# Key transposes in order, preparation and loads most of a batch ahead, attention up to 2.2 batches ahead

## The chip, the cores and the metric

The kernel runs on one core of one Trainium2 chip. The metric is the device time of one execution in microseconds; for the kernel before, three runs are shown, and their median is 276.2 us.

## The reference

Eight batches of 576 tokens and 8 heads of 64 numbers go through a pooled attention, and its output, 4608 tokens of 512 numbers, through a layer of eight experts of which each token uses one.

```python
# q, k, v: (8, 8, 576, 64)
k_p = k.reshape(B, H, 72, 8, D).mean(axis=3)         # keys and values pooled by 8: 72 groups
v_p = v.reshape(B, H, 72, 8, D).mean(axis=3)
attn = softmax(q @ k_p.T / sqrt(D))
x = (attn @ v_p) as rows of tokens, 4608 x 512
logits = (x / |x|) @ (expert_emb / |expert_emb|).T / tau
expert_idx = argmax(logits); gate_w = softmax(logits)[expert_idx]
out[t] = gate_w * (relu(x[t] @ w1[e]) @ w2[e])       # e = expert_idx[t]; w1 512 x 1024, w2 1024 x 512
```

## The kernel before, in words

All of a batch's tokens are multiplied with the weights of one expert, the one that the routing finds most often; a loop at the end repairs batches in which tokens chose others, and on this data it runs no round. So the work of batch b is: load its inputs, prepare them, do the attention, find the expert, load that expert's two weights, and do the expert layer (the FFN).

**Inputs** (`load_qkv`): keys, queries and values are loaded by three transfers in GpSimd's DMA queue, which also turns float32 into fp16. The pool `inp` has two buffers of each, so the inputs of batch b+2 can be loaded only when those of b have been used. **Weights** (`load_w`): two transfers of 1 MB (as fp16) in the same queue, three buffers each.

**Preparation**, all on VectorE. Keys (`kproc`): two additions, a transpose in blocks of 32x32, and a last addition that leaves `kT`, the pooled keys. The transpose (line 163) writes its result so that the two halves of a pooled group come to lie side by side, and the last addition (line 168) adds neighbours. Queries (`qtr`): two transposes. Values (`vadd`): three additions, which leave `vpx`.

**Attention**: `score` is 8 matmuls and two exponentials on ScalarE, four times a batch; `pv` is 48 small matmuls, and `xtr` normalizes and transposes their result on VectorE into `xt_all`, three times a batch. `square` on ScalarE, `sumsq` on GpSimd and `ssq` on TensorE form the tokens' norms; `gate_steps` makes the gate of it (a power on GpSimd, then VectorE and an exponential). `route` and `expert` find the expert's index, which GpSimd reads into a register before it can issue the weights' loads.

**The expert layer** (`ffn_steps`): 8 steps `hgrp` (w1, 8 matmuls each, ReLU on ScalarE, or on VectorE for w = 1 and 5), then 8 steps `yblk` and one `ylast` (w2, then the gate's scaling and the stores on SP's queue).

**The order** is written out by hand; each engine works through its instructions in the order in which the program names them. After a prologue, the program goes through the steps of the expert layers. A step at place x (batch number plus the done part of the layer) is preceded by all attention steps whose place is less than `lead(x)`. The places are numbers in `attn_steps`: batch plus 0.00 for the keys, 0.16 to 0.40 for the scores, and so on to 0.97 for the expert. `lead(x)` is x plus 1.5, growing to 1.7. The prologue holds all the attention of batch 0 and about half of that of batch 1.

In the profiles, names of buffers are the program's: `k` is the transposed key tile `k4`, `pa` any of the four PSUM tiles, `w` the weights, `at` the exponentials, `x_sb` and `xt_all` the attention's output.

## Time and profile before

| | |
|---|---|
| runs shown | 275.04, 276.2, 277.79 us; median 276.2 |
| profiled execution | 274.75 us, span 273.1 us, mean granted TensorE clock 0.882 |
| busy, share of the span | TensorE matmul 189.7 us (69%), VectorE 184.8 (68%), ScalarE 103.1 (38%), GpSimd 68.8 (25%) |
| DMA | 40.81 MB, mean 149 GB/s |

Busy times are averages over the whole span. An engine with 68% may still hold up the others in every batch, which is seen only in stretches of one batch and in the chain of waits: that chain is followed back from the last instruction, at each step to what released it. Adjacent pieces of it are on the path that set the end. The granted clock is TensorE's, as a share of full speed.

### The profile page before, as it was taken

To read this page: it belongs to the slowest core of one execution; us is meant where nothing else is said; L and a number is where in the kernel's file an instruction comes from. 1 tells how busy PE (TensorE), PEld (TensorE's weight loads), DVE (VectorE), ACT (ScalarE), POOL (GpSimd) and SP (SyncE) were. 2 spreads that over 40 slices of the span, in tenths; PEclk is the share of its full clock that TensorE was granted. 3 is DMA by queue.
4 is the path that set the end of the run, shared out by engine and by line. 5 is a ranking of instruction groups with operands and counts; after the bars stand their busy time and mean duration, and the time that the engine had idled before them with its cause. 6 is when DMAs were issued, how large, how long until landed. Compare 5 with 4: busy or idle time off the path is not lost.

```text
span 273.1 us, 6241 instructions
## 1 busy us (share of the span) xinstructions
PE 189.7 (69%) x2614; PEld 111.0 (41%) x2615; DVE 184.8 (68%) x353; ACT 103.1 (38%) x180; POOL 68.8 (25%) x75
## 2 busy tenths in 40 slices
PE   0144356682999189963999099927997599999930
PEld 0123234451268023750467035712475147758510
DVE  3969973559379963999299946997399929624110
ACT  2033513261427234371627053533427152815310
POOL 8204064150010900155012801081013301341000
PEclk9999997597799759995999779975999599999995
DMA  5998999991032899549985899479963954397340
GB/s 102 204 186 133 208 200 205 210 187 30 4 84 91 151 209 184 176 72 205 216 158 137 170 216 212 132 123 209 209 176 52 203 99 136 49 197 193 99 131 20
DMA packets 19582, 40.81 MB, mean 149 GB/s; under 512 B 2520, under 2 KB 8152, under 8 KB 18528
## 3 DMA queue, kind: packets, MB, share of 16 engines
q0 software_dynamic: 14096, 30.94, 62.0%
q1 hardware_dynamic: 5116, 8.86, 9.7%
q10 hardware_dynamic: 340, 0.59, 0.7%
q8 instruction: 21, 0.34, 0.5%
q14 instruction: 9, 0.07, 0.1%
HBM read 61.88 MB, written 9.44 MB: 261 GB/s over the span
## 4 chain that ended last, share of the span: by engine, by line
PE 57%; DVE 34%; ACT 2%; DMA 2%; issue 1%; ACTq 0%; POOLq 0%
PE pa L408 25%; PE pa L390 17%; DVE k L163 8%; DVE kT L168 6%; PE pa L203 5%; DVE qT L177 4%; PE pa L223 4%; PE pa L431 3%; DVE xt_all L240 2%; DVE x_sb L237 2%; DMA kk<-in_k_dram 2%; PE pa L276 2%; DVE kk L158 2%; DVE hT L399 2%; ACT at L209 2%; DVE ks L161 1%
## 5 line engine op out<-in xcount | busy, mean ns | idle before, releaser
L408 PE MATMUL pa<-w,hT 128*128 128x512 f16 x256 | 71.2, 427 | 0.0
L390 PE MATMUL pa<-xt_all,w 128*128 128x288 f16 x512 | 70.5, 294 | 0.0
L209 ACT ACTIVATE at<-pa 72x576 f16<-72x576 f32 x64 | 37.3, 642 | 81.1 <-PE pa L203 81.0
L203 PE MATMUL pa<-qT,kT 32*72 32x288 f16 x256 | 19.2, 386 | 57.9 <-DVE qT L177 57.3
L390 PEld LDWEIGHTS <-w 128*128 128x128 f16 x512 | 48.9, 100 | 14.8 <-issue 1.9
L408 PEld LDWEIGHTS <-hT 128*128 128x128 f16 x256 | 24.6, 105 | 36.2 <-issue 17.1
L397 ACT ACTIVATE hT<-pa 128x576 f16<-128x576 f32 x48 | 30.2, 646 | 18.9 <-PE pa L390 18.6
L203 PEld LDWEIGHTS <-kT 32*72 32x72 f16 x256 | 7.1, 132 | 72.3 <-DVE qT L177 45.1
L253 POOL TENSOR_TENSOR sq<-sq 128x1152 bf16<-128x1152 bf16 (+1 forms) x16 | 29.7, 1858 | 17.8 <-ACT sq L248 9.9
L349 POOL TENSOR_TENSOR ssq<-ssq,half_c 128x5 f32<-128x5 f32 x8 | 9.6, 1195 | 96.6 <-DVE ssq L265 96.6
L421 DVE TENSOR_SCALAR y_sb<-pa,gm 128x512 f32<-128x512 f32 x16 | 11.8, 735 | 32.1 <-PE pa L408 32.1
L240 DVE STREAM_TRANSPOSE xt_all<-x_sb 128x768 f16<-128x768 f16 x24 | 23.5, 979 | 0.8
L419 ACT ACTIVATE y_sb<-pa,gm 128x512 f32<-128x512 f32 x16 | 11.0, 688 | 34.4 <-DVE y_sb L421 29.0
L237 DVE TENSOR_TENSOR x_sb<-pa,rc 128x768 f16<-128x768 f32 x24 | 23.0, 957 | 0.8
L248 ACT ACTIVATE sq<-xt_all 128x576 bf16<-128x576 f16 x32 | 20.5, 677 | 6.8 <-DVE xt_all L240 6.8
L163 DVE STREAM_TRANSPOSE k<-ks 128x576 f16<-128x576 f16 x8 | 21.8, 2720 | 0.3
L177 DVE STREAM_TRANSPOSE qT<-qq 128x1152 f16<-128x1152 f16 x16 | 21.2, 1349 | 0.0
L100 POOL DMA_DIRECT2D w<-in_moe_w_dram x8 | 5.0, 621 | 61.7 <-DVE kk L158 38.8
L399 DVE TENSOR_SCALAR hT<-pa 128x576 f16<-128x576 f32 x16 | 11.8, 738 | 11.0 <-PE pa L390 11.0
L223 PE MATMUL pa<-vpx,at 72*32 72x65 f16 x1152 | 16.7, 205 | 2.7 <-ACT at L209 2.0
L223 PEld LDWEIGHTS <-at 72*32 72x32 f16 x1152 | 12.8, 102 | 8.9 <-issue 6.1
L235 DVE RECIPROCAL rc<-pa 128x12 f32<-128x12 f32 x24 | 5.3, 222 | 15.6 <-PE pa L223 15.5
(84 smaller groups left out, 156.7 us busy)
## 6 DMA issues: line engine op xcount, KB each, us to landing
w<-in_moe_w_dram POOLq DMA_DIRECT2D x16, 1024.0 KB, 10.8
out_dram<-y_sb SPq DMA_DIRECT2D x30, 256.0 KB
kk<-in_k_dram POOLq DMA_DIRECT2D x8, 576.0 KB, 14.4
vv<-in_v_dram POOLq DMA_DIRECT2D x8, 576.0 KB, 21.1
qq<-in_q_dram POOLq DMA_DIRECT2D x7, 576.0 KB, 17.4
out_dram<-y_sb SPq DMA_DIRECT2D x15, 64.0 KB
qq<-in_q_dram POOLq DMA_DIRECT2D x2, 288.0 KB, 8.3
out_dram<-y_sb ACTq DMA_DIRECT2D x2, 256.0 KB
```

What stands on the lines that cost most here:

```text
L163: nc.vector.transpose(out=k4.rearrange("p w r (i m) -> p m w r i", m=T // 4), in_=ks.rearrange("p m (w r i) -> p m w r i", w=2, r=2))
L177: nc.vector.transpose(out=qT.rearrange("p w r (t i) -> p t w r i", i=16), in_=qq.rearrange("p t (w r i) -> p t w r i", w=2, r=2))
L203: nc.tensor.matmul(out=pS[a // 2][0:G, (a % 2) * 512:(a % 2) * 512 + HALF], lhsT=kT[rows, w, r, :], rhs=qT[rows, w, r, :], start=(w == 0), ...
L209: nc.scalar.activation(out=at, in_=pS[i][0:G].rearrange("g (a c) -> g a c", a=2)[:, :, 0:HALF], func=AF.Exp, scale=escale)
L223: nc.tensor.matmul(out=px[ts(a, 32), c0:c0 + D + 1], lhsT=st['at', half, r, a // 2][:, a % 2, ts(blk, 32)], rhs=st['vpx'][:, 2 * a + r, 0: ...
L237: nc.vector.tensor_tensor(out=x_sb, in0=pxv[:, :, :, 0:D], in1=rc.unsqueeze(3).to_broadcast([128, 2, 6, D]), op=ALU.mult)
L240: nc.vector.transpose(out=xt_all[:, b].rearrange("p w (t l) -> p t w l", l=32)[:, ts(u, 6)], in_=x_sb.rearrange("p b j d -> p (b j d)").re ...
L248: nc.scalar.activation(out=st['sq'][:, w], in_=xt_all[:, b, w], func=AF.Square)
L253: nc.gpsimd.tensor_tensor(out=sq[:, 0:n], in0=sq[:, 0:n], in1=sq[:, n:2 * n], op=ALU.add)
L390: nc.tensor.matmul(out=ph[:, half * 512:half * 512 + HALF], lhsT=w1v[:, kk, w // 2, w % 2, :], rhs=xt()[:, kk, ts(half, HALF)], start=(kk ...
L397: nc.scalar.activation(out=dst, in_=src, func=AF.Relu)
L408: nc.tensor.matmul(out=py, lhsT=st['hT'][:, w // 2, w % 2, ts(c, 128)], rhs=w2[:, w // 2, w % 2, :], start=(w == 0), stop=(w == 7))
```

## The change

The diff, without a few lines that only follow from it (new bounds of loops and blank lines):

```diff
-    LEAD = 1.7
+    LEAD = 2.2
@@ kproc
-            k4 = att.tile([128, 2, 2, 2 * G], FP16, name="k4")
-            nc.vector.transpose(
-                out=k4.rearrange("p w r (i m) -> p m w r i", m=T // 4),
-                in_=ks.rearrange("p m (w r i) -> p m w r i", w=2, r=2))
+            k4 = att.tile([128, T // 4, 2, 2, 16], FP16, name="k4")
+            nc.vector.transpose(out=k4.rearrange("p m w r i -> p (m w r i)"),
+                                in_=ks.rearrange("p m d -> p (m d)"))
             kT = att.tile([128, 2, 2, G], FP16, name="kT")
-            k42 = k4.rearrange("p w r (g s) -> p w r g s", s=2)
-            nc.vector.tensor_tensor(out=kT, in0=k42[:, :, :, :, 0], in1=k42[:, :, :, :, 1],
-                                    op=ALU.add)
+            kTv = kT.rearrange("p w r (i m) -> p (w r) i m", i=8)
+            k4v = k4.rearrange("p m w r (i s) -> p (w r) i m s", s=2)
+            for dst, a, b_ in ((slice(0, 4), (slice(0, 8, 2), 0), (slice(1, 8, 2), 0)),
+                               (slice(4, 5), (slice(8, 9), 0), (slice(0, 1), 1)),
+                               (slice(5, 9), (slice(1, 9, 2), 1), (slice(2, 9, 2), 1))):
+                nc.vector.tensor_tensor(out=kTv[:, :, :, dst], in0=k4v[:, :, :, a[0], a[1]],
+                                        in1=k4v[:, :, :, b_[0], b_[1]], op=ALU.add)
@@ qtr
-            qT = att.tile([128, 2, 2, TH * 16], FP16, name="qT")
+            qT = att.tile([128, 2, 2, TH * 16], FP16, name="qT", bufs=4)
@@ expert
             weights[b] = load_w(e_val)
-            if b + 2 < B:
-                load_qkv(b + 2)
@@ places of the steps (attn_steps)
-        K = [(0.00, kproc)]
-        Q = [(0.07, lambda: qtr(0)), (0.18, lambda: qtr(1))]
-        V = [(0.24, lambda: vadd(0)), (0.30, lambda: [vadd(1), vadd(2)])]
-        SC = [(0.16 + 0.08 * i, lambda h=i // 2, r=i % 2: score(h, r)) for i in range(4)]
-        P = [(0.50 + 0.11 * u, lambda u=u: pv(u)) for u in range(3)]
-        X = [(0.505 + 0.11 * u, lambda u=u: xtr(u)) for u in range(3)]
-        R = [(0.92, lambda: route(0, NC)), (0.97, lambda: expert(list(range(NC))))]
-        A = [(0.80 + 0.04 * w, lambda w=w: square(w)) for w in range(4)]
-        A += [(0.99, sumsq)]
+        def more():
+            if b + 2 < B:
+                load_qkv(b + 2)
+        V = [(-0.80, lambda: vadd(0)), (-0.73, lambda: [vadd(1), vadd(2)])]
+        K = [(-0.64, kproc)]
+        Q = [(-0.52, lambda: qtr(0)), (-0.40, lambda: qtr(1))]
+        L = [(-0.36, more)]
+        SC = [(0.28 + 0.12 * i, lambda h=i // 2, r=i % 2: score(h, r)) for i in range(4)]
+        P = [(0.74 + 0.12 * u, lambda u=u: pv(u)) for u in range(3)]
+        X = [(0.745 + 0.12 * u, lambda u=u: xtr(u)) for u in range(3)]
+        R = [(1.10, lambda: route(0, NC)), (1.16, lambda: expert(list(range(NC))))]
+        A = [(1.02 + 0.05 * w, lambda w=w: square(w)) for w in range(4)]
         if b < 2:
-            R = [(0.5, lambda: route(0, 1)), (0.5, lambda: expert([0])),
-                 (0.85, lambda: route(1, 4)), (0.90, recount)]
+            R = [(0.87, lambda: route(0, 1)), (0.92, lambda: expert([0])),
+                 (1.10, lambda: route(1, 4)), (1.16, recount)]
@@ gate_steps
         def norm():
-            st['emit_ssq']()
...
-        return [norm, prob, gate]
+        return [st['sumsq'], st['emit_ssq'], norm, prob, gate]
@@ hgrp
-            if w % 4 != 1:
+            if w != 5:
                 nc.scalar.activation(out=dst, in_=src, func=AF.Relu)
@@ the prologue and the merge with the expert layers
+        def lead(pos):
+            return pos + min(1.2 + 0.25 * pos, LEAD)
         run(a0['K'], a0['Q'][:1], a0['S'][:2], a0['V'])
         emb_transposed(4)
-        run(a0['P'][:1], a0['X'][:1], a0['R'][:2], a0['Q'][1:], a0['S'][2:], a1['K'],
-            a0['P'][1:2], a0['X'][1:2], a1['Q'][:1], a0['P'][2:], a0['X'][2:], a1['S'][:2],
-            a1['V'], a0['R'][2:], a0['A'])
-        run(a1['P'][:1], a1['X'][:1], a1['R'][:2])
...
+        run(a0['P'][:1], a0['X'][:1], a0['R'][:2], a0['Q'][1:], a0['S'][2:], a0['L'],
+            a0['P'][1:2], a0['X'][1:2], a1['K'], a0['P'][2:], a0['X'][2:], a1['Q'][:1],
+            a0['R'][2:], a0['A'], a1['V'][:1])
+        fill(psum()[:, 0:512], 12)
+        astream = [(1 + pos, f) for g in (a1['V'][1:], a1['Q'][1:], a1['S'], a1['L'], a1['P'],
+                                          a1['X'], a1['R'], a1['A']) for pos, f in g]
...
-                astream.append((b + (1.6, LEAD + 0.12, LEAD + 0.24)[i], f))
+            places = (min(b + 1.5, lead(b) + 0.1), min(b + 1.8, lead(b + 0.28)),
+                      min(b + 1.83, lead(b + 0.31)), lead(b + 0.36), lead(b + 0.43))
+            astream += list(zip(places, gate_steps(b)))
-        def lead(pos):
-            return pos + min(1.5 + 0.2 * pos, LEAD)
```

The transpose of the keys now writes its result in the order in which it reads it, and three additions (128, 32 and 128 elements a partition) pick the two halves of each group out of it. Values, keys and queries of a batch are prepared 0.4 to 0.8 batch earlier in the order, values first; scores and what follows come later in the numbers, but `lead` grows to 2.2, so they stand further ahead of the expert layer. The loads of batch b+2 come after the last query transpose of batch b instead of after the expert's weights. The sum of squares and the norm have places of their own. Batch 1's scores and what follows, its expert included, leave the prologue; 12 matmuls of 512 columns that compute nothing come ahead of the first expert layer. One of the two ReLU steps of a layer moves from VectorE to ScalarE.

On VectorE, at the change from one batch to the next (`ix` is the expert's index, `kk`, `ks`, `k4`, `kT` the keys, `vv`, `vpx` the values; line numbers of the changed kernel are higher by 4 from the key additions on), the order before was:

```order
L306 MAX_INDEX ix_2257<-mx_2255,pa_2248 1x8
L307 TENSOR_SCALAR eb_all_91<-pa_2248,mx_2255 128x8
L319 TENSOR_SCALAR pos_all_92<-pa_2248 1x8
L158 TENSOR_TENSOR kk_1799<-kk_1799 128x9x128
L161 TENSOR_TENSOR ks_2284<-kk_1799 128x576
L163 STREAM_TRANSPOSE k4_2286<-ks_2284 128x9x64
L168 TENSOR_TENSOR kT_2288<-k4_2286 128x288
L399 TENSOR_SCALAR hT_2094<-pa_2290 128x576
L177 STREAM_TRANSPOSE qT_2300<-qq_1798 128x18x4x16
L177 STREAM_TRANSPOSE qT_2336<-qq_1798 128x18x4x16
L186 TENSOR_TENSOR vv_1800<-vv_1800 72x8x256
L186 TENSOR_TENSOR vv_1800<-vv_1800 72x8x128
```

Keys, queries and values were those of the batch whose scores came next. In the changed kernel the same place reads:

```order
L310 MAX_INDEX ix_2718<-mx_2716,pa_2709 1x8
L311 TENSOR_SCALAR eb_all_91<-pa_2709,mx_2716 128x8
L321 TENSOR_SCALAR pos_all_92<-pa_2709 1x8
L190 TENSOR_TENSOR vv_1985<-vv_1985 72x8x256
L190 TENSOR_TENSOR vv_1985<-vv_1985 72x8x128
L194 MEMSET vpx_2760 72x8x2
L195 TENSOR_TENSOR vpx_2760<-vv_1985 72x8x64
L158 TENSOR_TENSOR kk_1984<-kk_1984 128x9x128
L161 TENSOR_TENSOR ks_2788<-kk_1984 128x576
L163 STREAM_TRANSPOSE k4_2790<-ks_2788 128x576
L172 TENSOR_TENSOR kT_2792<-k4_2790 128x32x4
L172 TENSOR_TENSOR kT_2792<-k4_2790 128x32
```

The values now come right behind the expert's index, the keys behind them, and both belong to the batch after the one whose scores come next.

On GpSimd, after the prologue's loads (`sq` are the squares, `ix` the index of batch 1, `w1` and `w2` its weights, `kk`, `qq`, `vv` inputs), the order before was:

```order
L93 DMA kk_282<-in_k_dram 128x2304
L94 DMA qq_281<-in_q_dram 128x2304
L95 DMA vv_283<-in_v_dram 72x8x512
L253 TENSOR_TENSOR sq_500<-sq_500 128x1152
L253 TENSOR_TENSOR sq_500<-sq_500 128x576
L311 TENSOR_LOAD ix_577
L311 ISA x2
L100 ISA
L100 DMA w1_590<-in_moe_w1_dram 128x4096
L103 ISA
L103 DMA w2_591<-in_moe_w2_dram 128x4x1024
L93 DMA kk_595<-in_k_dram 128x2304
```

The inputs ahead of batch 1's weights were those of batch 2, and batch 3's came behind the weights. Now:

```order
L257 TENSOR_TENSOR sq_471<-sq_471 128x1152
L257 TENSOR_TENSOR sq_471<-sq_471 128x576
L355 TENSOR_TENSOR ssq_620<-ssq_620,half_c_97 128x5
L93 DMA kk_650<-in_k_dram 128x2304
L94 DMA qq_649<-in_q_dram 128x2304
L95 DMA vv_651<-in_v_dram 72x8x512
L315 TENSOR_LOAD ix_821
L315 ISA x2
L100 ISA
L100 DMA w1_834<-in_moe_w1_dram 128x4096
L103 ISA
L103 DMA w2_835<-in_moe_w2_dram 128x4x1024
```

Three batches of inputs have been issued ahead of the weights of batch 1 since those of batch 0's expert: batches 2 and 3 above these rows, and batch 4 in them.

## Rows read from the trace of the kernel before

**Rows 1.** Windows by period: length, busy PE, PEld, DVE, ACT, POOL; clock, DMA, GB/s.

```profile
118.26:147.60 29.34, 22.32 (x327) 12.92 (x326) 23.48 (x43) 12.84 (x24) 8.27 (x8) 0.88 0.83 171
147.60:177.19 29.59, 22.75 (x327) 13.00 (x326) 23.36 (x42) 12.49 (x23) 8.27 (x8) 0.88 0.84 174
```

**Rows 2.** Chain of waits, prologue and 118 to 128: start us, us, what.

```profile
11.14 0.46 DVE kT L168
...
118.26 0.68 DVE kk L158
...
119.46 2.73 DVE k L163
...
122.21 3.19 DVE kT L168
...
126.06 1.30 DVE qT L177
...
127.40 0.70 PE pa L203 x6
```

**Rows 3.** Timeline, 117 to 135: start, us, engine, line, operation [idle before <-releaser].

```profile
117.92 0.15 DVE L306 FIND_INDEX8 ix<-mx,pa 1x8 uint32<-1x8 f32 x1
...
119.35 0.64 POOL L100 DMA_DIRECT2D w<-in_moe_w_dram  x1 [7.58 <-DVE kk L158]
...
122.69 3.84 POOL L253 TENSOR_TENSOR sq<-sq 128x1152 bf16<-128x1152 bf16 x2
...
127.40 0.70 PE L203 MATMUL pa<-qT,kT 32*72 32x288 f16 x8 [6.85 <-DVE qT L177]
...
128.04 1.89 PE L408 MATMUL pa<-w,hT 128*128 128x512 f16 x4
...
130.46 1.90 PE L408 MATMUL pa<-w,hT 128*128 128x512 f16 x8
```

**Rows 4.** Windows of 10 us, columns as in rows 1.

```profile
10.00:20.00 10.00, 3.86 (x79) 2.74 (x80) 7.83 (x14) 2.26 (x4) 0.00 (x0) 1.00 1.07 200
120.00:130.00 10.00, 3.15 (x21) 0.97 (x22) 9.93 (x7) 2.39 (x5) 6.44 (x6) 0.68 0.97 176
...
160.00:170.00 10.00, 10.00 (x163) 4.78 (x162) 4.38 (x9) 4.72 (x8) 0.51 (x1) 0.95 1.08 216
```

**Rows 5.** Chain of waits, whole span: first w1 matmuls (L390) of layers, and others.

```profile
34.73 0.81 PE pa L223 x30
...
38.75 1.96 PE pa L390 x8
...
80.34 1.09 PE pa L390 x8
...
170.03 1.09 PE pa L390 x8
...
228.22 1.09 PE pa L390 x8
...
261.91 0.69 ACT y_sb L419
```

**Rows 6.** Groups by form, 147.55 to 177.15: busy us, mean ns | idle before.

```profile
L240 DVE STREAM_TRANSPOSE xt_all<-x_sb 128x768 f16<-128x768 f16 x3 | 2.9, 979 | 0.1
...
L163 DVE STREAM_TRANSPOSE k<-ks 128x576 f16<-128x576 f16 x1 | 2.7, 2723 | 0.0
...
L399 DVE TENSOR_SCALAR hT<-pa 128x576 f16<-128x576 f32 x2 | 1.5, 732 | 0.0
...
L357 DVE TENSOR_TENSOR lg<-lg,rn 128x40 f32<-128x40 f32 x1 | 0.2, 199 | 0.0
```

**Rows 7.** Groups by form, whole span: the scaling of the expert embedding.

```profile
L513 DVE TENSOR_SCALAR emb_h<-emb,emb_n 8x512 f16<-8x512 f32 x1 | 1.4, 1353 | 0.1
```

**Rows 8.** The page's DMA queues: packets, MB, share of 16 engines' span.

```profile
q0 software_dynamic: 14096, 30.94, 62.0%
q1 hardware_dynamic: 5116, 8.86, 9.7%
```

More of the change, by code (lines that the diff above doesn't have):

```diff
@@ L325, in recount @@
             present(pc)
-        st['emit_ssq'] = ssq
         routes[b] = st
-        K = [(0.00, kproc)]
-        Q = [(0.07, lambda: qtr(0)), (0.18, lambda: qtr(1))]
-        V = [(0.24, lambda: vadd(0)), (0.30, lambda: [vadd(1), vadd(2)])]
-        SC = [(0.16 + 0.08 * i, lambda h=i // 2, r=i % 2: score(h, r)) for i in range(4)]
-        P = [(0.50 + 0.11 * u, lambda u=u: pv(u)) for u in range(3)]
-        X = [(0.505 + 0.11 * u, lambda u=u: xtr(u)) for u in range(3)]
-        R = [(0.92, lambda: route(0, NC)), (0.97, lambda: expert(list(range(NC))))]
-        A = [(0.80 + 0.04 * w, lambda w=w: square(w)) for w in range(4)]
-        A += [(0.99, sumsq)]
+        def more():
[10 more added lines that the diff above has]
+        A = [(1.02 + 0.05 * w, lambda w=w: square(w)) for w in range(4)]
         if b < 2:
-            R = [(0.5, lambda: route(0, 1)), (0.5, lambda: expert([0])),
-                 (0.85, lambda: route(1, 4)), (0.90, recount)]
-        return dict(K=K, Q=Q, V=V, S=SC, P=P, X=X, R=R, A=A)
+            R = [(0.87, lambda: route(0, 1)), (0.92, lambda: expert([0])),
+                 (1.10, lambda: route(1, 4)), (1.16, recount)]
+        st['sumsq'], st['emit_ssq'] = sumsq, ssq
+        return dict(K=K, Q=Q, V=V, S=SC, L=L, P=P, X=X, R=R, A=A)
     def gate_steps(b):
@@ L523, in run @@
                     f()
+        def lead(pos):
+            return pos + min(1.2 + 0.25 * pos, LEAD)
         run(a0['K'], a0['Q'][:1], a0['S'][:2], a0['V'])
         emb_transposed(4)
-        run(a0['P'][:1], a0['X'][:1], a0['R'][:2], a0['Q'][1:], a0['S'][2:], a1['K'],
-            a0['P'][1:2], a0['X'][1:2], a1['Q'][:1], a0['P'][2:], a0['X'][2:], a1['S'][:2],
-            a1['V'], a0['R'][2:], a0['A'])
-        run(a1['P'][:1], a1['X'][:1], a1['R'][:2])
-        astream = []
-        for i, f in enumerate([*a1['Q'][1:], *a1['S'][2:], *a1['P'][1:2], *a1['X'][1:2],
-                  *a1['P'][2:], *a1['X'][2:], *a1['R'][2:], *a1['A']]):
-            astream.append((1.5 + 0.02 * i, f[1]))
+        run(a0['P'][:1], a0['X'][:1], a0['R'][:2], a0['Q'][1:], a0['S'][2:], a0['L'],
[4 more added lines that the diff above has]
+                                          a1['X'], a1['R'], a1['A']) for pos, f in g]
         for b in range(B):
@@ L538 @@
                     astream += [(b + pos, f) for pos, f in g]
-            for i, f in enumerate(gate_steps(b)):
-                astream.append((b + (1.6, LEAD + 0.12, LEAD + 0.24)[i], f))
+            places = (min(b + 1.5, lead(b) + 0.1), min(b + 1.8, lead(b + 0.28)),
+                      min(b + 1.83, lead(b + 0.31)), lead(b + 0.36), lead(b + 0.43))
+            astream += list(zip(places, gate_steps(b)))
         astream = sorted(astream, key=lambda s: s[0])
-        def lead(pos):
-            return pos + min(1.5 + 0.2 * pos, LEAD)
         j = 0
```

## The prediction

> **What bounds the kernel now.** First the stretches of one period each (between two first key additions): 29.34 and 29.59 us, in which the trace has TensorE busy for 22.3 to 22.8 us, VectorE for 23.4 to 23.5, and the DMA engines for shares of 0.83 and 0.84, that is 24.4 and 24.9 us [rows 1]. No engine fills the period, so something makes them take turns. The chain of waits says what: from 118.26 to 127.40 it lies on VectorE alone, which adds and transposes the keys of a batch (the transpose 2.73 us, the last addition 3.19 us, the same addition 0.46 us in the prologue) and then its queries, and only then do the scores run [rows 2]. The timeline shows the price on TensorE, 6.85 us idle before the score matmuls, and behind the gap four 128x512 matmuls in 1.89 us, where eight take 1.90 soon after: it restarts at the lower of its two clocks (1.2 against 2.4 GHz), and the granted clock of 120 to 130 us is 0.68 [rows 3, 4]. That is about 7 + 1.4 us of each period. The timeline also says why the addition grows from 0.46 to 3.19: from 122.69 on GpSimd adds squares, two instructions in 3.84 us, and the addition ends only when the first is over [rows 3].
>
> Seen by the starts of the expert layers in the chain (first w1 matmuls), the span falls into a start to 38.75, layer 0 to 80.34, layers 1 to 3 to 170.03, layers 4 and 5 to 228.22, layers 6 and 7, with hardly any attention beside the last, to 261.91, and an end of 10.5 us from the last evacuation's end at 262.6 to 273.1 [rows 5].
>
> **The change, part by part.** Key transpose in order: before, it wrote 2-byte elements 18 bytes apart, 2723 ns for 576 elements; the transpose of the attention output, which writes runs of 32, takes 979 ns for 768, 1.27 ns each [rows 6]. So 576 in order cost 0.73 us by that row, 2.72 if the order of writing is not the reason. I take 0.75: less 1.97 us a batch. A gain beyond this has no row.
>
> Three key additions for one: 128, 32 and 128 elements. A 40-element addition takes 199 ns [rows 6], nearly all fixed, and the old one 0.46 us for 288 elements [rows 2]; three together are 0.75, plus 0.3 us over the unlocked old one. They now read with a step of 128 bytes. The nearest row for steps that long is the embedding scaling, 512 elements written 256 bytes apart in 1353 ns, or 2.6 ns each [rows 7], and the farthest the old transpose at 4.7; so the upper end is 288 x 4.7 + 0.45 = 1.8 us. I take 0.75 because those rows step on the write, and here only the read does. The Trainium skill, "SBUF — State Buffer", section "Door 1: The DMA port swizzle", speaks against this part: an access that enters a new 16-byte line each time pays for it, and the change would carry that cost from the transpose's writes to the additions' reads. By that rule the additions cost the 1.8, VectorE keeps 1 us more per batch, and the sum below becomes 2 to 5 us more.
>
> ReLU of w = 1 to ScalarE: VectorE loses one of 732 ns a batch [rows 6]; ScalarE gains about 0.65 on 12.8 of 29 us [rows 1], covered.
>
> Squares' sums and gate chain: the GpSimd work is the same 3.84 us, and it still comes right behind the weight DMAs in GpSimd's queue, which start 1.3 us after the expert index is found (118.07 to 119.35) [rows 3]. The sums then fall, some 2.7 us after the index, on the value and key additions that the change puts there. So the lock stays, at 2.4 (first instruction) to 3.8 us (both); nothing is booked as gained.
>
> VectorE per batch: 23.4 - 1.97 - 0.73 - 2.44 (the addition without its lock, 3.19 to 0.75) = 18.3, with the lock 20.7 to 22.1. TensorE: 22.5 less the restart of 1.4 = 21. DMA, unchanged in bytes: 24.4 to 24.9 us at share 1.0; the windows reach 0.97 to 1.08, at 176 to 216 GB/s [rows 4], so 23 to 25 us. Most of it is GpSimd's queue, 62.0% of the span against 9.7% for the stores [rows 8].
>
> Preparation ahead: keys and queries of a batch now stand 0.6 to 1 batch before their scores, so the 6.85 us wait goes while VectorE keeps up. The loads of inputs b+2 are issued right after the last query transpose of b, no longer behind the weights; GpSimd's queue waits there for VectorE, and behind it wait the norm's power and the next weights. Next late are therefore the weights: once the 7 us go, the DMA time of a batch exceeds both engines'.
>
> **The sum, by the stages above.** Start: the two key chains ahead lose 1.65 us each; batch 1's first values, output and routing (4 us of the chain, 34.73 to 38.75 [rows 5]) leave, and 12 filling matmuls of 512 columns (0.24 to 0.47 us each [rows 3], 2.9 to 5.7) come. 38.75 to **37**.
> Layer 0: its end is the arrival of batch 1's weights, which were fetched in the prologue and now wait for batch 1's route inside layer 0. Inputs 0 to 2 and one expert are 3 x 1.77 + 2.10 = 7.4 MB (from the tiles' sizes); at 200 GB/s from 1.4 us they land at 38.5 to 40. From there VectorE has values 2.3, keys 2.7, queries 2.6, one ReLU 0.7, the gate 1.5, two output blocks 4.4, route and count 1.5 = 15.7, and a lock of 2.4 to 3.8: 57 to 59.5. Issue 1.3, w1 of 1.05 MB 5.2: 64 to 66. **28**.
> Layers 1 to 3: the DMA queue sets them, 23 to 25.6 (5.05 MB at the saturated windows' mean of 197 GB/s). Taken 23.5: **70.5**.
> Layers 4 and 5: all inputs are loaded soon after layer 4 begins, weights alone are 10.5 us a batch; VectorE and TensorE set 21 to 23. Taken 22: **44**.
> Layers 6 and 7: as before, 262.6 - 228.2 = **34.4**. The end: **10.5**.
> Together 224.4 against a span of 273.1. The profiled execution is 274.75, 1.65 over its span, and the median of the three runs shown is 276.2, 1.45 over that: 224.4 + 1.65 + 1.45 = 227.5, forecast **228 us**. Its own bounds: start 1.5, layer 0 3, layers 1 to 3 up to 6 more or 4.5 less, layers 4 and 5 3 each way: 216 to 241.
>
> **Rivals.** (A) The DMA queue is no bound, TensorE is, 21 us for six batches: 37 + 126 + 34.4 + 10.5 + 3.1 = **211**. Against it: 24.4 to 24.9 us of DMA per batch at share 1.0. Chance 0.08.
> (B) VectorE becomes the bound: transpose at 2.72, additions at 1.8, the lock whole: 18.3 + 1.97 + 1.05 + 3.8 = 25.1, and 1 for waits on TensorE's results, 26 for five batches, layer 0 at 30: 37 + 30 + 130 + 48 = **245**. For it: one in-order engine carries preparation and output blocks, and at 22 it is close to the others already. 0.20.
> (C) The change does not do what it says: loads waiting in GpSimd's queue hold up the weights, so the wait only changes its owner and five batches stay at 29.5: 37 + 30 + 147.5 + 48 = **262**. Against it: weights are issued about a batch before use. 0.05.
> (D) Slower: VectorE takes up the values of batch b+2 before they have landed and blocks there, with output blocks, route, weight issue and loads behind it, so that the batch becomes one chain: values 2.3, keys with lock 6.5, queries 2.6, output 6.6, route 1.5, issue 2.7, both weights 10.5 = 32.7 us. Six batches: 37 + 196 + 48 = **281**. It decides where a period passes 31.9 us ((276.2 - 37 - 48) / 6), that is where inputs land more than about 1.5 batches after their issue. At 176 GB/s, the lowest saturated row, a batch's 5.05 MB take 28.7, so it does not follow from any row here. 0.04.
>
> **Numbers.** The forecast has 0.63. The range **216 to 247** holds its own bounds and (B), leaving out (A) below and (C) and (D) above. A measurement here tells 1% from no change. Faster by over 1%: all but (D) and an outlying (C), 0.94; within 1% 0.02; slower 0.04.
>
> **What would show it.** Right: a key transpose near 0.75 us and three additions of 0.2 to 0.3; no wait of scores for the query transposes; first w1 matmuls near 37, 65, 88, 112, 135, 157, 179 and 197 us, those of layers 1 to 4 released by the weights' DMA, with the DMA share at 0.95 or more between them; the sums of squares still beside a stretched key or value addition. Wrong: VectorE over 95% busy with TensorE waiting on it (B); the weights issued late in a layer, behind a load that waits for VectorE (C); VectorE idle on the values' DMA (D); layer starts 21 us apart with the DMA share well under 0.9 (A). The likeliest mistake is the DMA term: a rate 5% off moves the middle three layers by 3.5 us, and a late batch 1 moves everything behind it.

## The result, and the profile after

The changed kernel takes **259.5 us** (median of 4 runs, 257.6 to 260.2) where the kernel before, beside it on the same chip, takes 277.0: a ratio of 0.937, with a 95% interval of 0.929 to 0.944. The forecast was 228, with a range of 216 to 247. The direction was right, and the gain, 17.5 us, is about a third of the 48 expected.

The profiled execution has a span of 258.1 us. By stages (a layer runs from its first w1 matmul to that of the next, read from the timeline of TensorE; us):

| | start | layer 0 | layers 1, 2, 3 | layers 4, 5 | rest | span |
|---|---|---|---|---|---|---|
| before | 38.6 | 41.7 | 30.7, 29.0, 30.0 | 30.1, 28.1 | 44.9 | 273.1 |
| forecast | 37 | 28 | 23.5 each | 22 each | 44.9 | 224.4 |
| after | 37.5 | 35.3 | 33.2, 30.4, 33.5 | 23.5, 21.4 | 43.3 | 258.1 |

The start, layers 4 and 5 and the rest came within 2 us of the forecast. Layer 0 is 7.3 us over it, and layers 1 to 3 are 26.6 over it, which makes them 7.4 us slower than before. Windows of layers 1 to 5 (columns as in [rows 1], to which they answer):

```profile
72.80:106.00 33.20, 26.28 (x341) 14.41 (x341) 26.66 (x50) 15.39 (x27) 9.15 (x10) 0.85 0.83 161
106.00:136.40 30.40, 25.27 (x428) 14.63 (x428) 25.61 (x49) 14.60 (x25) 11.48 (x11) 0.89 1.01 210
136.40:169.90 33.50, 25.68 (x407) 14.52 (x406) 24.71 (x50) 14.08 (x26) 6.62 (x5) 0.90 0.63 137
169.90:193.40 23.50, 22.55 (x329) 13.29 (x326) 21.36 (x43) 12.71 (x23) 6.27 (x5) 0.93 0.64 134
193.40:214.80 21.40, 20.98 (x332) 12.69 (x331) 11.34 (x31) 13.23 (x25) 6.22 (x5) 1.00 0.72 156
```

VectorE, third of the busy times, has 24.7 to 26.7 us in layers 1 to 3 and 21.4 and 11.3 in layers 4 and 5. In layer 3 the DMA share is 0.63, so no transfer rate explains 33.5 us there. Layers 1 to 3 together, before and after:

```profile
80.30:170.00 89.70, 68.70 (x978) 39.12 (x977) 70.53 (x124) 37.99 (x67) 24.80 (x25) 0.87 0.81 167
72.80:169.90 97.10, 77.23 (x1173) 43.56 (x1173) 76.98 (x148) 44.07 (x78) 27.24 (x26) 0.88 0.82 168
```

The three layers hold 1173 matmuls where they held 978, so more of the attention stands in them, and TensorE is busy in them for 77.2 us, where the forecast had 21 a layer, 63 in all. The granted clock, 0.88, is no higher than before; in layer 5, at 1.00, TensorE is busy for 21.0 us.

The parts that were costed one by one came as forecast. Groups by form over the whole span, the answer to [rows 6]:

```profile
L195 DVE TENSOR_TENSOR vpx<-vv 72x512 f16<-72x512 f16 x8 | 10.6, 1323 | 0.1
L158 DVE TENSOR_TENSOR kk<-kk 128x1152 f16<-128x1152 f16 x8 | 9.1, 1132 | 0.1
L172 DVE TENSOR_TENSOR kT<-k 128x128 f16<-128x128 f16 x16 | 7.8, 490 | 0.3
L163 DVE STREAM_TRANSPOSE k<-ks 128x576 f16<-128x576 f16 x8 | 6.2, 778 | 0.3
```

The key transpose takes 778 ns (forecast 0.75 us; 2720 before). The chain in layer 0, which answers to [rows 2], has the three additions together in 0.77 us, and ahead of them the wait of layer 0, for the values of batch 2:

```profile
23.16 21.76 DMA vv<-in_v_dram
...
44.95 1.23 DVE vv L190
...
48.55 0.79 DVE k L163
...
49.36 0.77 DVE kT L172 x3
50.12 1.29 DVE qT L181
```

The Trainium skill, "SBUF — State Buffer", section "Door 1: The DMA port swizzle", says that each access that crosses to a new 16-byte line pays a penalty; by that rule the prediction had the additions cost 1.8 us. The trace has 0.77, so here the measurement decides against using the rule for these reads. (Their step is 256 bytes in the two longer additions, which take every second of the rows of 128 bytes, and not 128 as the prediction has it.)

What went wrong in layers 1 to 3 stands in the timeline, 120 to 130 and 152 to 154 (the expert layer's matmuls, L390 and L408 before, are L396 and L414 here; start, us, engine, line, operation [idle before <- releaser]; the answer to [rows 3]):

```profile
120.41 2.75 DVE L195 TENSOR_TENSOR vpx<-vv 72x512 f16<-72x512 f16 x1
120.49 4.47 POOL L257 TENSOR_TENSOR sq<-sq 128x1152 bf16<-128x1152 bf16 x2
...
123.86 1.42 DVE L161 TENSOR_TENSOR ks<-kk 128x576 f16<-128x576 f16 x1
...
128.09 0.71 DVE L427 TENSOR_SCALAR y_sb<-pa,gm 128x512 f32<-128x512 f32 x1
...
128.84 0.69 ACT L425 ACTIVATE y_sb<-pa,gm 128x512 f32<-128x512 f32 x1 [4.53 <-DVE y_sb L427]
...
129.57 0.85 PE L227 MATMUL pa<-vpx,at 72*32 72x65 f16 x48 [3.37 <-ACT y_sb L425]
...
152.42 0.33 ACT L366 ACTIVATE lg<-lg,lnxs 128x40 f32<-128x40 f32 x1 [6.29 <-DVE lg L363]
...
153.33 1.23 PE L207 MATMUL pa<-qT,kT 32*72 32x288 f16 x8 [5.03 <-ACT at L213]
```

VectorE works in order: values (stretched to 2.75 us beside GpSimd's squares), keys (1.42 us for an addition that takes 0.46 undisturbed), the transposes, and only then, at 128.09, the evacuation `y_sb` of one half of a w2 result (the copy out of PSUM that scales it by the gate). The stretching of VectorE's additions beside GpSimd's is what the prediction calls the lock. ScalarE's evacuation of the other half waited 4.53 us for it, and TensorE 3.37 us for a free PSUM tile. From 146 on it is the gate chain that stands behind the keys: ScalarE waits 6.29 us for the gate's logits, the exponentials of the scores stand behind it, and TensorE waits 5.03 us. The list of waits (engine, line, waited for: us in sum, times, longest):

```profile
ACT y_sb L425 <- DVE y_sb L427: 40.5, 10, 5.9
...
ACT lg L366 <- DVE lg L363: 16.1, 6, 6.3
...
PE pa L207 <- DVE qT L181: 13.1, 2, 11.2
...
PE pa L207 <- ACT at L213: 5.5, 3, 5.0
...
PE pa L227 <- ACT y_sb L425: 3.4, 1, 3.4
...
PEld L396 <- DMA w<-in_moe_w_dram: 0.9, 1, 0.9
```

The wait of scores for queries, 57.3 us in 9 times before, is down to 2 times, both in the start (in layer 0 the scores still wait 6.1 us for VectorE, released by `ssq`, behind the late values and the preparation). The wait on weights that the forecast put in its place is under 1 us in the whole span.

### The profile page after: what moved, and what is told of

The parts are those of the page before. It is cut to its first block, busy times and chain, and to the rows that moved or that the text cites. A ratio compares the mean times of both kernels' runs of the same rounds, so it can differ in the third digit from the quotient of the medians.

```text
span 258.1 us, 6297 instructions
## 1 busy us (share of the span) xinstructions
PE 190.4 (74%) x2626; PEld 111.5 (43%) x2627; DVE 169.7 (66%) x361; ACT 107.4 (42%) x188; POOL 70.7 (27%) x75
## 4 chain that ended last, share of the span: by engine, by line
PE 37%; DVE 37%; DMA 12%; issue 4%; ACT 4%; POOL 1%; POOLq 0%; ACTq 0%
PE pa L396 15%; DMA vv<-in_v_dram 12%; PE pa L414 12%; DVE x_sb L241 6%; DVE xt_all L244 5%; DVE vv L190 4%; DVE vpx L195 4%; PE pa L227 3%; DVE kT L172 3%; DVE kk L158 3%; PE pa L437 2%; DVE qT L181 2%; PE pa L207 2%; PE pa L280 2%; DVE y_sb L427 2%
## 5 line engine op out<-in xcount | busy, mean ns | idle before, releaser
L396 PE MATMUL pa<-xt_all,w 128*128 128x288 f16 x512 | 74.2, 300 | 2.6 <-ACT y_sb L425 2.1
L414 PE MATMUL pa<-w,hT 128*128 128x512 f16 x256 | 66.6, 402 | 0.1
L396 PEld LDWEIGHTS <-w 128*128 128x128 f16 x512 | 49.9, 102 | 21.2 <-issue 6.0
L213 ACT ACTIVATE at<-pa 72x576 f16<-72x576 f32 x64 | 37.5, 643 | 27.8 <-PE pa L207 27.7
L403 ACT ACTIVATE hT<-pa 128x576 f16<-128x576 f32 x56 | 35.5, 648 | 16.6 <-PE pa L396 16.2
L207 PE MATMUL pa<-qT,kT 32*72 32x288 f16 x256 | 16.9, 330 | 30.1 <-DVE qT L181 13.1
L414 PEld LDWEIGHTS <-hT 128*128 128x128 f16 x256 | 23.3, 101 | 29.3 <-issue 8.3
L257 POOL TENSOR_TENSOR sq<-sq 128x1152 bf16<-128x1152 bf16 (+1 forms) x16 | 31.6, 1976 | 4.5 <-issue 3.8
L244 DVE STREAM_TRANSPOSE xt_all<-x_sb 128x768 f16<-128x768 f16 x24 | 23.5, 978 | 0.8
L190 DVE TENSOR_TENSOR vv<-vv 72x2048 f16<-72x2048 f16 (+1 forms) x16 | 15.1, 947 | 9.3 <-DMA vv<-in_v_dram 9.0
L227 PE MATMUL pa<-vpx,at 72*32 72x65 f16 x1152 | 15.6, 207 | 5.6 <-ACT y_sb L425 3.4
L227 PEld LDWEIGHTS <-at 72*32 72x32 f16 x1152 | 12.6, 104 | 14.6 <-issue 11.9
L427 DVE TENSOR_SCALAR y_sb<-pa,gm 128x512 f32<-128x512 f32 x16 | 11.7, 730 | 9.9 <-PE pa L414 9.9
L280 PE MATMUL pa<-enT,xt_all 128*128 128x8 f16 (+1 forms) x192 | 6.7, 172 | 14.8 <-DVE xt_all L244 14.6
```

Source lines behind the costliest of these rows:

```text
L190: nc.vector.tensor_tensor(out=vv[:, :, 0:n], in0=vv[:, :, 0:n], in1=vv[:, :, n:2 * n], op=ALU.add)
L207: nc.tensor.matmul(out=pS[a // 2][0:G, (a % 2) * 512:(a % 2) * 512 + HALF], lhsT=kT[rows, w, r, :], rhs=qT[rows, w, r, :], start=(w == 0), ...
L213: nc.scalar.activation(out=at, in_=pS[i][0:G].rearrange("g (a c) -> g a c", a=2)[:, :, 0:HALF], func=AF.Exp, scale=escale)
L227: nc.tensor.matmul(out=px[ts(a, 32), c0:c0 + D + 1], lhsT=st['at', half, r, a // 2][:, a % 2, ts(blk, 32)], rhs=st['vpx'][:, 2 * a + r, 0: ...
L244: nc.vector.transpose(out=xt_all[:, b].rearrange("p w (t l) -> p t w l", l=32)[:, ts(u, 6)], in_=x_sb.rearrange("p b j d -> p (b j d)").re ...
L257: nc.gpsimd.tensor_tensor(out=sq[:, 0:n], in0=sq[:, 0:n], in1=sq[:, n:2 * n], op=ALU.add)
```

## The experiments

Each is timed in three rounds beside the kernel before (medians 275.8 to 276.9); ratios are to that kernel. Layer times come from the one profiled execution, read as above.

**E1, the key transpose alone.** The kernel before with the change's part of `kproc` (the diff is cut to its transpose) and nothing else.

```diff
-            nc.vector.transpose(out=k4.rearrange("p w r (i m) -> p m w r i", m=T // 4), ...)
+            nc.vector.transpose(out=k4.rearrange("p m w r i -> p (m w r i)"), ...)
```

> The kernel before with the in-order key transpose and the three additions alone, all places as they were. Theory Q (what the change gained is mostly this): the chain at each batch's head loses 2.72 - 0.78 us of transpose and gains 0.3 us of additions, 1.6 us in each of 8 batches, on the path: 277 - 13 = 262 to 266 us. Rival (the gain comes from preparing and loading ahead): the addition only waits longer for GpSimd's squares, 271 to 276.

252.9 us, ratio 0.915 [0.910, 0.920]: below both expectations, and faster than the whole change. Its windows of layers 1 to 5, columns as before:

```profile
75.90:100.50 24.60, 22.10 (x327) 12.84 (x325) 21.03 (x44) 12.61 (x23) 8.97 (x9) 0.93 0.74 150
100.50:123.80 23.30, 20.80 (x328) 12.67 (x327) 20.62 (x44) 12.56 (x23) 8.96 (x9) 1.00 0.94 199
123.80:148.50 24.70, 20.99 (x327) 12.76 (x325) 19.23 (x44) 12.72 (x23) 8.25 (x9) 1.00 0.96 202
148.50:175.80 27.30, 22.46 (x328) 13.01 (x327) 19.28 (x44) 12.68 (x23) 8.21 (x9) 0.94 1.01 210
175.80:205.70 29.90, 22.96 (x328) 13.04 (x327) 22.97 (x44) 12.64 (x23) 6.25 (x6) 0.89 0.71 156
```

Layers 1 to 3 have the period that was forecast for the whole change, 23 to 25 us, but not for its reason: in E1 no wait of TensorE for weights shows. The wait for the queries is 2.50 us in each of these layers (6.85 before) though nothing was moved ahead. The shorter chain did it, and it took the lock off the key addition too, as the timeline of E1 shows: the additions end before GpSimd begins, and in layers 1 and 2 the lock falls on the values, for which no scores wait. Layer 5 shows the reverse: there GpSimd begins beside the key additions, they take 4.44 us, the scores wait 6.66, and the layer takes 29.9.

```profile
109.75 0.77 DVE L172 TENSOR_TENSOR kT<-k 128x128 f16<-128x128 f16 x3
...
112.16 4.62 POOL L257 TENSOR_TENSOR sq<-sq 128x1152 bf16<-128x1152 bf16 x2
...
112.53 0.44 PE L207 MATMUL pa<-qT,kT 32*72 32x288 f16 x8 [2.50 <-DVE qT L181]
...
113.65 3.67 DVE L190 TENSOR_TENSOR vv<-vv 72x2048 f16<-72x2048 f16 x2
...
186.01 4.44 DVE L172 TENSOR_TENSOR kT<-k 128x128 f16<-128x128 f16 x3
186.37 3.75 POOL L257 TENSOR_TENSOR sq<-sq 128x1152 bf16<-128x1152 bf16 x2
...
192.46 0.70 PE L207 MATMUL pa<-qT,kT 32*72 32x288 f16 x8 [6.66 <-DVE qT L181]
```

**E5, the rest of the change without the key transpose.** The changed kernel with E1's hunk taken back.

> The changed kernel with the old key transpose and its one addition: everything of the change but the in-order transpose. Theory Q (the transpose alone gained 24 us, the new places and loads lose 6 to 7 us of it): VectorE's queue, late as it is in layers 1 to 3, gets 1.65 us a batch more: 270 to 284 us, no faster than before by more than 2%. Rival (each part gains, and they overlap): 260 to 268.

271.6 us (runs from 269.6 to 274.6), ratio 0.983 [0.975, 0.990], as the first theory had it. Alone the new order gains some 4 us; put on top of E1 it loses 6.6 (252.9 to 259.5).

**E2, E3, E10: two ways to free the evacuations, and both.** E2 sums the squares on TensorE, so that GpSimd's additions, and with them the lock and about 4 us between squares and gate, are gone (diff shortened, without `sumsq`, which does nothing now):

```diff
 def ssq():
-    nc.tensor.matmul(out=pq[rows, c:c + 1], lhsT=st['sq'][:, 0, cols(c)], rhs=ones_b, start=True, stop=True)
+    for w in range(4):
+        nc.tensor.matmul(out=pq[rows, c:c + 1], lhsT=st['sq'][:, w, cols(c)], rhs=ones_b,
+                         start=(w == 0), stop=(w == 3))
```

> The changed kernel, but the squares are summed by TensorE (four accumulating matmuls for each one before, 18 more tiny matmuls a batch) and GpSimd adds nothing. Theory Q (VectorE's queue is late in layers 1 to 3, because GpSimd's squares hold up the value and key additions, and PSUM evacuations and the gate stand behind them): 12 us of stretched additions go from layers 1 to 3, 3 more behind; 246 to 252 us. Rival D (the DMA queue sets layers 1 to 3, as predicted): 257 to 262. Rival L (the order on VectorE alone, locked or not): 255 to 259.

E3 leaves the lock and does all w2 evacuations on ScalarE (the first of two places is shown):

```diff
-                if i % 2:
+                if True:
                     nc.scalar.activation(out=y_sb, in_=py, func=AF.Copy, scale=g)
```

> The changed kernel, but all of the scaled evacuations of w2's result run on ScalarE, which then does not wait for VectorE's half of the pair; the work is the same, VectorE loses 1.9 us a batch and ScalarE gains as much. Theory Q: TensorE's waits for PSUM tiles that end with these evacuations (1.5 + 2.6 + 2.0 + 1.5 + 3.4 + 0.5 us in layers 0 to 2, and part of the slow clock behind them) go: 246 to 253 us. Rival D: 257 to 261. Rival L2 (ScalarE is held anyway by the gate's exponential): 255 to 259.

> The changed kernel with the sums of squares on TensorE (no lock) and all w2 evacuations on ScalarE, the gate chain left at its place. Theory Q (two views of one queue: with either remedy, 250.4 and 252.1, the evacuations no longer wait, so both together add little, and the weights' DMA is next): 247 to 250, TensorE's waits on weights 3 to 6 us in sum. Rival (the two remedies are independent and add, 9.1 and 7.4 us): 242 to 245.

E2 250.4 us (ratio 0.901 [0.893, 0.909]), E3 252.1 (0.907 [0.900, 0.913]), E10 247.2 (0.894 [0.889, 0.899]). The parts, 9.1 and 7.4 us, give 12.3 together, 4.2 less than their sum: in part the same wait seen from two ends. In E2 the value and key additions are back at their undisturbed times, and TensorE now waits for weights:

```profile
L158 DVE TENSOR_TENSOR kk<-kk 128x1152 f16<-128x1152 f16 x8 | 6.0, 744 | 0.2 <-DMA kk<-in_k_dram 0.2
...
L195 DVE TENSOR_TENSOR vpx<-vv 72x512 f16<-72x512 f16 x8 | 3.4, 421 | 0.1
```
```profile
PE pa L394 <- DMA w<-in_moe_w_dram: 4.2, 3, 2.7
```

E10 has layers 1 to 3 at 27.5, 26.3 and 30.4 us, 84.2 together:

```profile
72.50:156.70 84.20, 72.51 (x1245) 43.27 (x1246) 58.98 (x132) 47.96 (x86) 14.10 (x18) 0.96 0.93 196
```

12.9 of the 26.6 us are explained, and 13.7 are left. Of the 12.9, TensorE's idle time is 8.2 (19.9 to 11.7) and its busy time 4.7, at a granted clock of 0.96 instead of 0.88.

**E6, the gate chain earlier, and E7, with E2 and E3.**

```diff
-                      min(b + 1.83, lead(b + 0.31)), lead(b + 0.36), lead(b + 0.43))
+                      min(b + 1.83, lead(b + 0.31)), min(b + 1.92, lead(b + 0.36)),
+                      min(b + 1.97, lead(b + 0.43)))
```

> The changed kernel, but the two steps of the gate on VectorE that stood after the key preparation stand ahead of the value additions (places b+1.92 and b+1.97 where they were b+2.3 to b+2.6). The work is the same. Theory G (ScalarE, in order, waits 16 us for the gate's logits behind the key additions, and the exponentials of the scores and TensorE behind it): the 5.0 us wait of the scores in layer 3 and part of those in layers 2 and 4 go, 251 to 256 us. Rival (only PSUM evacuations count): 258 to 261.

> The changed kernel with three edits together: squares summed on TensorE, w2's evacuations all on ScalarE, the early gate. Theory Q: what VectorE's lateness costs is gone, and the weights' DMA sets layers 1 to 3 at 25 to 27 us: 241 to 247 us. Rival (the DMA queue holds already at e2's and e3's level): 248 to 252.

E6 265.2 us (0.962 [0.957, 0.968]), E7 252.2 (0.913 [0.906, 0.920]): a miss, 5.7 and 5.0 us slower than without the edit. The 5 us wait of the scores is gone, but the gate now stands ahead of the attention's output on VectorE, and route and index come later (the index of batch 3 at 121.7 us in E6, 117.7 in the changed kernel): TensorE's wait of the route for the output's transpose grew from 14.6 us to

```profile
PE pa L280 <- DVE xt_all L244: 24.0, 9, 6.4
```

**E9, preparation of batches 3 and 4 moved** from beside the w2 steps to beside the w1 steps.

```diff
+        d = {3: 0.27, 4: 0.52}.get(b, 0)
+        V, K, Q, L = ([(p + d, f) for p, f in g] for g in (V, K, Q, L))
```

> The changed kernel with one thing moved: value, key and query preparation (and the loads behind it) of batches 3 and 4 from beside the w2 steps of layers 0/1 and 1/2 to beside the w1 steps of layers 1 and 2; those of batches 5 to 7 stay. Theory P (the loss of layers 0 to 2 is the place: locked additions ahead of the two output blocks' evacuations on VectorE): the waits of TensorE on ScalarE's y_sb shrink to under 1 us in layers 0 and 1, layers 0 to 2 (98.9 us of the changed kernel) lose 4 to 8, total 251 to 256. Rival R (the lock costs wherever the preparation stands, VectorE's time is what counts): total 258 to 261. Rival D (loads now come too late): slower than 261, with values or keys waiting for DMA.

267.4 us, 0.965 [0.958, 0.972]: the rival on loads. The loads of batch 5 and 6 follow the moved steps, and VectorE stood before the values, which the chain shows with 25.5 us from issue to landing:

```profile
127.81 25.52 DMA vv<-in_v_dram
```

So it does not test the place by itself, and shows what a later load costs: VectorE blocked on values, for 4.2 us, as in the prediction's rival (D), though not in the kernel that it was written for. That wait lies in layer 3; most of the loss is in layer 2, 37.3 us instead of 30.4, and how that comes about stays open.

**E4 and E15, fewer bytes.** Queries of batches 2 to 7 are not loaded, those of batches 0 and 1 stand in for them, in the changed kernel (E4) and in E10 (E15).

```diff
+        if b > 1:
+            loads[b] = (loads[b - 2][0], kk, vv)   # kk, vv loaded as before, no load of qq
```

> The changed kernel, but the queries of batches 2 to 7 are not loaded; those batches use the queries of batches 0 and 1. 0.59 of 5.05 MB a batch less in the DMA queue, the work of the engines is the same. Rival D (the DMA queue is the bound of layers 1 to 3): 3 us a batch, 246 to 252 us. Theory Q: within 3 us of the changed kernel, 256 to 260.

> The changed kernel with the sums of squares on TensorE and all w2 evacuations on ScalarE (247.2), and the queries of batches 2 to 7 not loaded (those of batches 0 and 1 are used again; the output of these batches is not the reference's). That takes about 0.59 MB as fp16, 3 us at 196 GB/s, off the queue for each batch. Theory D (with VectorE's waits gone the DMA queue sets layers 1 to 3: 84.2 us for 16.5 MB at share 0.93): these layers fall by 6 to 12 us, TensorE's waits on weights (3.4 us) go, total 236 to 241. Rival E (the engines' order sets them): 245 to 248, as the same cut did next to nothing in the changed kernel itself (259.5 to 257.5).

E4 257.5 us (0.928 [0.923, 0.934]), with layers 1 to 3 at 97.1 as in the changed kernel: there the DMA queue is no bound. Layer 0 fell from 35.3 to 32.7. E15 240.4 (0.863 [0.855, 0.870]), the total that its theory gave, but not where: layer 0 went from 34.1 to 30.1 us and layers 1 to 3 from 84.2 to 83.2. Bytes ahead of layer 0 cost 4 us in that order (2.6 in E4's); they do not explain layers 1 to 3 in that order.

**E12 and E13, scores to expert a quarter batch earlier**, on E10 and on the changed kernel.

```diff
+        SC, P, X, R, A = ([(p - 0.25, f) for p, f in g] for g in (SC, P, X, R, A))
```

> The changed kernel with the sums of squares on TensorE, all w2 evacuations on ScalarE, and scores, output, squares, route and expert a quarter of a batch earlier. Theory W (the expert's index of batches 1 to 3 comes too late in the new order: 93.8 us for weights wanted at 106, which then need 10 us to land): TensorE's waits on weights, 3.4 us in the kernel without the shift, go, and the time falls from 247.2 to 240 to 244. Rival D (the DMA queue is full there and earlier issue lands no earlier; layers stay at 23 to 27): 246 to 249. Rival V (scores and output blocks crowd the preparation on VectorE in layer 0): above 249.

> The changed kernel with scores, output, squares, route and expert a quarter of a batch earlier, the lock and the evacuations as they are. Theory Q (locked additions ahead of evacuations are the main loss; the late index only shows once they are gone): 254 to 260. Rival W (the late index is the main loss): 245 to 251.

E12 251.6 us (0.911 [0.904, 0.917]), E13 261.9 (runs from 258.4 to 263.3; 0.948 [0.940, 0.957]): neither gains. In E12 TensorE's wait on weights at the start of layer 2 fell from 3.1 us to 0.9, and the time did not. A late index (93.8 us, weights wanted at 106) is not the main loss.

**E16 and E17, the lead capped at 1.7**, in the changed kernel and in E12.

```diff
-    LEAD = 2.2
+    LEAD = 1.7
```

> The changed kernel with lead capped at 1.7 (as before) instead of 2.2; all else as changed. Theory S (layers 1 to 3 are long because 1.25 batches of attention stand in each, and VectorE, at 25 to 27 us busy, has none to spare there while it has in layers 5 to 7): layers 2 and 3 fall from 30.4 and 33.5 to 26 to 29, layers 5 and 6 grow by 2 to 4, total 252 to 257. Rival R (the same work only moves to later layers, and the index, now half a batch before its use, comes too late): 259 to 264.

> The same cap of 1.7, with the squares summed on TensorE, all w2 evacuations on ScalarE, and scores to expert a quarter batch earlier, so that the index keeps its distance (251.6 without the cap). Theory S: layers 2 and 3 (27.3 and 30.6 us) fall to 23 to 25, total 243 to 247. Rival R (work only moves): 250 to 253.

E16 266.3 us (0.960 [0.954, 0.966]), slower than the changed kernel and above both expectations. The work moved, as the rival has it: layer 3 fell from 33.5 us to 28.8, but layers 4 and 6 grew from 23.5 to 29.3 and from 16.4 to 21.3. Its wait of ScalarE for VectorE's half has grown, and scores wait behind it (2.0 us once in the changed kernel, now 15.5 in four waits):

```profile
ACT y_sb L425 <- DVE y_sb L427: 46.2, 13, 6.6
...
PE pa L207 <- ACT y_sb L425: 15.5, 4, 4.5
```

E17 241.9 us (0.873 [0.869, 0.877]), 9.8 below E12, the shortest time of all runs of the whole computation. Layers 1 to 4 of E17:

```profile
73.20:99.50 26.30, 22.75 (x440) 13.66 (x440) 21.79 (x46) 16.91 (x30) 5.86 (x8) 1.00 0.97 205
99.50:126.70 27.20, 22.64 (x343) 13.51 (x343) 17.39 (x40) 14.81 (x26) 4.48 (x6) 0.88 1.05 218
126.70:149.60 22.90, 22.86 (x344) 13.69 (x345) 14.74 (x36) 13.87 (x24) 2.56 (x3) 0.91 0.93 189
149.60:171.10 21.50, 21.25 (x346) 12.90 (x345) 17.17 (x40) 14.84 (x26) 2.55 (x3) 1.00 0.75 164
```

Layer 3 fell from 30.6 us to 22.9 and layer 4 from 24.8 to 21.5, where the lead had still been growing; layers 6 and 7 grew from 16.6 to 18.1 and from 26.9 to 28.8. Layer 2 did not move (27.3 to 27.2), against the expectation: there, and in layer 1, the DMA share is 0.97 to 1.05, and TensorE waits 2.1 and 4.6 us for weights at their ends. That looks like the DMA bound that had been forecast; no run took bytes out of E17 to test it.

```profile
PE pa L395 <- DMA w<-in_moe_w_dram: 6.7, 2, 4.6
```

**E8, E11, E14, built on E1.** E8 is E1 with E2's sums; E11 is E8 with the loads of batch b+2 right behind the values of b; E14 is E8 with E3's evacuations, seven of eight ReLUs on ScalarE, and scores 0.06 batch later (output, squares and route 0.01 to 0.04). The diffs are shortened.

```diff
+        if 1 < b < B - 2:                                            # E11
+            V += [(0.31, lambda: load_qkv(b + 2))]
-            if w % 4 != 1:                                           # E14
+            if w != 5:
-        SC = [(0.16 + 0.08 * i, ...                                  # E14
+        SC = [(0.22 + 0.08 * i, ...
```

> The kernel before with the in-order key transpose, and the squares summed on TensorE, so that GpSimd no longer holds up VectorE's additions. Theory D' (with the transpose alone the DMA queue is the bound of layers 1 to 4, share 0.97 to 1.08 and 24.5 us a layer): within 4 us of the transpose alone, 248 to 253 us. Rival (the lock still sets the period): 240 to 246.

> The kernel before with the in-order key transpose, the squares' sums on TensorE, and the loads of batch b+2 (b = 2 to 5) issued right after the values of b instead of after b's expert weights. In the same kernel without the earlier loads (246.7) the DMA share is 0.27 in layer 0 and 0.96 to 0.98 from there to layer 4, and layers 3 and 4 take 27.1 and 26.5 us where layers 1 and 2 take 23.7 and 24.2. Theory D (the DMA queue is the bound from layer 2 on, so work moved into its idle time is gained): DMA share above 0.6 in layer 0, layers 3 and 4 at 23.5 to 25, total 240 to 244. Rival (the loads only delay the weights behind them, or VectorE and TensorE, 19.2 and 21.3 us busy, set 24 with their waits on the queries anyway): 245 to 249.

> The kernel before with the in-order key transpose, the squares' sums on TensorE, all w2 evacuations and seven of eight ReLUs on ScalarE, and the scores 0.06 batch later (output, squares and route 0.02 to 0.04 later). In the version without the last three (246.7) TensorE waits about 2.5 us in each of layers 1 to 4 for the second query transpose. Theory P (VectorE's turn at keys and queries is still the only wait; less work ahead of it and later scores close it): 241 to 244. Rival D (the DMA share is 0.96 to 0.98 in three of the layers, so nothing is gained there): 245 to 248.

E8 246.7 us (0.896 [0.890, 0.901]), E11 245.9 (0.888 [0.881, 0.895]), E14 242.8 (0.879 [0.872, 0.886]). The order before, with five small edits, is as good as the new one with its remedies (E17: the intervals overlap). In layers 1 to 3, where the remedies took 12.9 us off the changed kernel, they give the order before next to nothing: 72.6 us in E1, 72.7 in E8, and in E14

```profile
70.40:142.30 71.90, 65.07 (x1034) 39.47 (x1031) 50.41 (x117) 44.39 (x79) 13.37 (x19) 1.00 0.88 184
```

So the loss that they end in those layers belongs to the new order. E11's earlier loads gave nothing that can be measured: layers 3 and 4 went from 24.8 and 27.1 us to 23.7 and 24.2, but layer 0 from 36.3 to 39.8, with TensorE's 428 matmuls in it busy for 32.4 us at a granted clock of 0.91 instead of 28.8 at 1.00. (E11's expectation counts E8's layers wrongly: 27.1 and 26.5 are layers 4 and 5, and layer 0 has a DMA share of 0.77, not 0.27.)

## Why the prediction was wrong, point by point

**Costs of single edits: right.** Key transpose (0.75 against 0.78), three additions (0.75 against 0.77), the lock still there, and falling on values and keys. Start, layers 4 and 5 and the end: right within 2 us; there the preparation has its room, and the forecast's period of 22 us holds, in layer 5 by TensorE alone (21.0 of 21.4 us), as hardly any preparation is left for VectorE (11.3 us).

**The step that failed** is the one on preparation ahead: "the 6.85 us wait goes while VectorE keeps up", and after it "Next late are therefore the weights". The wait went. But VectorE does not keep up in layers 1 to 3, so the term of 23.5 us a layer that "the DMA queue sets" measured 33.2, 30.4 and 33.5, and next late were not the weights but the evacuations and the gate, which stand behind the moved preparation in VectorE's queue. I had named VectorE's sum per batch (20.7 to 22.1 us with the lock) and compared it with TensorE's and the DMA's as if an engine below its period were free whenever it is asked; rival (B) counted the same sum, only higher. What was not asked is what is queued behind the moved instructions, and who waits for it. (By the places in `attn_steps` the preparation moved by 0.58 batch for queries to 1.04 for values, not by 0.4 to 0.8.) The 26.6 us over the forecast in layers 1 to 3 divide, in the order in which the experiments took them, into:

- 12.9 us: evacuations and gate behind stretched preparation (the changed kernel's 97.1 to E10's 84.2); this part is shown from both ends by E2 and E3;
- 7.8 us: too much attention in a layer (84.2 to E17's 76.4, with E12's shift; part of it moved to the last layers, and over the whole kernel E17 is 5.3 us below E10). The lead grows from 1.2 by 0.25 a layer, so each of layers 0 to 3 holds 1.25 batches of attention instead of one, as VectorE's instructions show (50, 49, 50 and then 43). I booked one batch's work for each. This shows only once the evacuations are free: E16 without the remedies is slower. The cap was not run on E10 without the shift, nor the two steps in the other order with every part apart, so the split between them is that of this sequence;
- 5.9 us: what is left (76.4 against 70.5), by its signs the DMA term, mis-sized at 23.5, though no run tests this; in E17's layers 1 and 2 it is 26.3 and 27.2 at the saturated share, above even the bound of 25.6, because more than one batch's bytes fall into them (26.3 us at 205 GB/s are 5.4 MB, 27.2 at 218 are 5.9).

**Layer 0**, 28 forecast, 35.3 measured. The values of batch 2 landed at 44.9, not at 38.5 to 40: their load, issued at 23.16, took 21.8 us, with batch 3's keys issued at 27.95 in the same queue, which I had not counted among the bytes. From 1.4 us to then the engines moved 186 GB/s, 8.1 MB, where I had 7.4 MB at 200 GB/s:

```profile
1.40:45.00 43.60, 19.82 (x306) 12.57 (x307) 25.49 (x58) 14.35 (x26) 15.58 (x22) 1.00 1.03 186
```

At the other end w1 was taken to land 5.2 us after its issue; its eight loads take 8.1 to 10.8, and batch 1's, issued at 63.12, held the weight load of layer 1 until 71.81.

```profile
DMA to landing us min/median/max: 8.1/8.7/10.8
```

With 0.59 MB a batch less, layer 0 is 4.0 us shorter in E15 and 2.6 in E4, so bytes are shown to be a part of the 7.3, and in E15 more than half. The last 1.0 us is the lock on values (2.47 us for an addition of 0.42) ahead of an evacuation, behind which layer 1's first matmul waited 1.5 us.

**The gain's owner.** I gave 2 us a batch to the transpose and the rest of the gain to the new order. E1 and E5 say the reverse: 24 us for the transpose alone, 4 for the order alone. The transpose stood at the head of the chain that TensorE waited for, so 1.94 us off it and 2.7 of the lock that it no longer meets, less 0.3 for the additions, are the 4.35 us by which the wait fell in layers 1 to 3 (6.85 to 2.50), and the restarts at the lower clock (the granted clock of layers 2 and 3 is 1.00 in E1, 0.88 and 0.89 before) came back with it.

**The rivals.** (A) did not show: TensorE sets 21.4 us in layer 5 alone. (B), 245, had the right engine by another mechanism, the sum and not the order: VectorE is busy for 74 to 84% of layers 1 to 3, where 95% was to show it. (C), 262, came nearest in time, by luck: the wait did change its owner, but the owner is not the weights, for which TensorE waited 0.9 us in all. (D) showed in part: VectorE waits for values for 7.9 us in layer 0, and for 4.2 in E9, but nowhere does a batch become one chain.

What stays open: whether E17's layers 1 and 2 are bound by the queue, and how much of their time a faster one would give, and whether the evacuations could stay on VectorE if only the places of the preparation were moved; E9, meant to show that, moved the loads as well.

## What to carry to other kernels

Moving work ahead on an in-order engine only changes who waits: list what stands behind it in that engine's queue (evacuations that free a buffer first of all) before calling it free. Try the edit that shortens the chain at its head alone; here it gave more than the whole package. And where a lead grows over the layers, each of them carries more than one batch of the moved work, so its period must be sized with that share.
